# Block 0 of a fused attention and SwiGLU kernel: four unused TensorE products between q's transposes and k^T v

## The chip, the cores and the metric

The kernel runs on one core of a Trainium2 chip, in one launch. The metric is the device time of that core in microseconds. Profile times are counted from the start of the profiled execution's span. The engines are TensorE (PE for its products and transposes, PEld for its weight loads), VectorE (DVE), ScalarE (ACT), GpSimd (POOL) and SyncE (SP), which issues most DMAs.

## The reference

It is a linear attention with a norm, followed by a SwiGLU feed-forward block on the same tokens.

```
q, k, v: (8 batches, 8 heads, 576 tokens, 64)
kv  = einsum('bhsd,bhse->bhde', k, v)
out = einsum('bhsd,bhde->bhse', q, kv)
rms = sqrt(mean(out * out, axis=-1) + 1e-6)
x   = (out / rms * g_norm) as 4608 tokens x 512        (heads side by side)
g, val = x @ w_gate, x @ w_val                         (512 x 1536 each)
y   = (g * sigmoid(g) * val) @ w_out                   (1536 x 512) -> 4608 x 512
```

## The kernel before

The 4608 tokens are worked on in nine blocks of 512. A block's attention part is an `Att` object and its feed-forward part an `Ffn` object. For each batch the kernel first makes the eight matrices k^T v; then a block of q is transposed, multiplied with them, normalised and transposed again, so that x lies with its 512 columns on the partitions for the feed-forward products. Block 0 does its feed-forward products plainly (`plain_up`, line 1018). The later blocks use a scheme with seven products in place of eight, from block 2 on applied twice over (lines 549 and 712). While a block's feed-forward part runs, the attention part of the next block is slipped in between.

The weights come in 36 pieces of 0.5 MB, as pairs of 32-bit words, and are turned into float32 by ScalarE (lines 146 and 160) and VectorE (lines 147, 152, 153 and 162) while block 0 runs. They share four load buffers (`ld`) with q, k and v, so that a load waits until its buffer has been read. SyncE issues these loads in order of the program.

Block 0's attention part has nothing to run beside. Its order on each engine is the order of the program, with a few ScalarE and VectorE steps placed by hand (`tc.issue_after`). The method `first` writes it out:

- `turn_q(0, ...)`, line 335: TensorE transposes the first two of q's four tiles (four transposes each). The first result goes to a tile of `b_psum` and is copied by VectorE to `qt[:, 0]` (line 339); the second goes to `c_psum` and is copied by ScalarE (line 337).
- `first_kv`, line 248: 36 products of 64 x 64 for the first four heads and 36 for the others, in two PSUM banks, from k and v as they land. ScalarE copies one bank (line 252), VectorE adds the other (line 111).
- `product(0)`, line 355: q times k^T v for two tiles, and the squares (ScalarE, line 366) and their sums (VectorE, line 367).
- `turn_q(1, ...)`: the other two tiles of q, the same way.
- `product(1)`: the same for them.
- `warm`, line 480: seven products of 128 x 512, the identity times the turned q tile `qt[:, 3]`, into one tile of `c_psum`. Nobody reads that tile.
- `root` (lines 373 to 385) and `scale` (line 113) on VectorE: the reciprocal root by three steps of iteration, and its multiplication with the product.
- `turn_x`, line 402: TensorE transposes the normalised x, ScalarE copies it with the gain (line 403).

After this `plain_up` goes through the twelve column tiles of w_gate and w_val.

A float32 product of TensorE shows as two rows in the profile, a float32 transpose as one. `c_psum` has two buffers that are used in turn, `b_psum` three, `m_psum` two and `a_psum` one.

## Time and profile before

| what | value |
| --- | --- |
| median of 4 runs | 1031.67 us (1030.37 to 1032.05) |
| the profiled execution's own time | 1031.43 us |
| its span | 1029.5 us, so 1.93 us lie around it |
| TensorE busy (products) | 1013.5 us, 98% of the span, 8570 rows |
| VectorE busy | 703.6 us, 68% |
| ScalarE busy | 230.1 us, 22% |
| GpSimd busy | 371.3 us, 36% |
| TensorE idle from 6.81 to 10.84 us | 4.03 us |
| TensorE busy between 36 and 114.5 us | 78.50 of 78.50 us |
| DMA engines' share between 36 and 114.5 us | 0.82 |

The busy times are of one profiled execution. A row of TensorE's timeline gives the start and the duration of a group of instructions, the line of the kernel, what is written and read, the shape, and how often; the bracket tells how long the engine sat idle before it and what ended that. Durations of single rows overlap, since products are pipelined: the distance between two starts says how fast they go, the duration holds the latency too.

### The profile page before, as it was taken

The numbers are of one execution on the slowest core, as the hardware profiler recorded it, in microseconds if no ns is written. First come the engines' busy times: TensorE is split into PE (matmuls) and PEld (weight loads), VectorE is DVE, ScalarE is ACT, GpSimd is POOL, SyncE is SP. The second block draws the span as 40 slices with busy tenths as digits, with TensorE's granted clock in tenths as the row PEclk, the third lists the DMA queues.
The fourth block names the chain that finished last, engine by engine and source line by source line (L and its number), as shares of the span: only waits on it lengthen the run. The fifth ranks groups of instructions, "written<-read, shape, count | busy, mean of one in ns | idle before, by whom it ended". The sixth has DMA issues, their size and how long they took to land.

```text
span 1029.5 us, 21440 instructions
## 1 busy us (share of the span) xinstructions
PE 1013.5 (98%) x8570; PEld 904.5 (88%) x8570; DVE 703.6 (68%) x1185; ACT 230.1 (22%) x359; POOL 371.3 (36%) x280
## 2 busy tenths in 40 slices
PE   6999999999999999999999999999999999999998
PEld 4544688888999989998999899988999999989997
DVE  2999796997766855585657576674669466856661
ACT  2765121222111211211112122111112111211110
POOL 0000543444035612562156304630455136513670
PEclk9999999999999999999999999999999999999999
DMA  8689614773778466855686468736872766066601
GB/s 216 207 257 266 122 28 128 194 217 79 204 208 242 84 139 205 247 127 114 194 243 162 69 205 240 198 53 186 244 196 47 174 193 192 22 165 207 189 30 41
DMA packets 252404, 168.15 MB, mean 163 GB/s; under 512 B 129169, under 2 KB 220433, under 8 KB 252305
## 3 DMA queue, kind: packets, MB, share of 16 engines
q1 hardware_dynamic: 225808, 163.37, 58.0%
q10 hardware_dynamic: 26432, 3.41, 2.0%
q8 instruction: 68, 1.11, 0.5%
q14 instruction: 32, 0.25, 0.1%
q0 software_dynamic: 64, 0.00, 0.0%
HBM read 138.02 MB, written 22.41 MB: 156 GB/s over the span
## 4 chain that ended last, share of the span: by engine, by line
PE 83%; DVE 8%; DMA 5%; SPq 1%; ACT 1%; issue 1%; DVEq 0%; ACTq 0%
PE b L712 26%; PE b L549 20%; PE c L712 13%; PE c L549 10%; PE a L712 6%; PE a L549 5%; DMA ld<-in_moe_w_out_dram 2%; PE m L355 1%; PE m L314 1%; SPq L281 1%; DVE r L153 1%; DMA h<-in_v_dram 1%; DMA ld<-in_v_dram 1%; DVE xi L112 1%; DVE r L147 1%
## 5 line engine op out<-in xcount | busy, mean ns | idle before, releaser
L111 POOL TENSOR_TENSOR r<-r 128x256 f32<-128x256 f32 (+1 forms) x105 | 110.7, 1061 | 309.5 <-DVE r L111 206.3
L111 DVE TENSOR_TENSOR r<-b,r 128x512 f32<-128x512 f32 (+1 forms) x273 | 162.0, 606 | 64.3 <-PE b L712 59.2
L112 POOL TENSOR_TENSOR t<-wo 128x512 f32<-128x512 f32 x81 | 116.9, 1467 | 190.8 <-DVE wo L111 106.0
L111 DVE TENSOR_TENSOR r<-c,r 128x512 f32<-128x512 f32 (+1 forms) x179 | 108.4, 617 | 94.7 <-PE c L712 55.6
L712 PE MATMUL b<-x,t 128*128 128x128 f32 x1092 | 151.0, 275 | 0.0
L712 PEld LDWEIGHTS b<-x,t 128*128 128x128 f32 x1092 | 136.5, 192 | 0.6
L111 DVE TENSOR_TENSOR r<-a,r 128x512 f32<-128x512 f32 (+1 forms) x99 | 62.4, 631 | 107.9 <-PE a L549 63.0
L712 PE MATMUL c<-xi,t 128*128 128x128 f32 x840 | 112.2, 275 | 0.4 <-DVE xi L111 0.4
L113 POOL TENSOR_TENSOR h<-r 128x1024 f32<-128x1024 f32 (+1 forms) x40 | 82.1, 2069 | 80.5 <-DVE r L111 72.8
L712 PEld LDWEIGHTS c<-xi,t 128*128 128x128 f32 x840 | 102.8, 192 | 0.5 <-DVE xi L111 0.5
L549 PE MATMUL b<-wo,h 128*128 128x256 f32 x432 | 99.5, 382 | 0.1
L549 PE MATMUL b<-t,h 128*128 128x256 f32 x432 | 96.9, 381 | 0.0
L549 PEld LDWEIGHTS b<-t,h 128*128 128x128 f32 x432 | 81.4, 190 | 11.3 <-issue 0.2
L549 PEld LDWEIGHTS b<-wo,h 128*128 128x128 f32 x432 | 80.0, 190 | 12.8 <-DVE h L113 2.5
L726 ACT COPY r<-b 128x512 f32<-128x512 f32 x63 | 36.9, 585 | 211.7 <-PE b L712 199.8
L712 PE MATMUL b<-xi,t 128*128 128x128 f32 x588 | 79.7, 276 | 0.0
L712 PEld LDWEIGHTS b<-xi,t 128*128 128x128 f32 x588 | 72.4, 192 | 0.0
L712 PE MATMUL b<-x,wg 128*128 128x128 f32 x336 | 52.7, 279 | 0.2 <-DVE x L112 0.2
L712 PE MATMUL b<-x,wv 128*128 128x128 f32 x336 | 51.4, 275 | 0.0
L549 PE MATMUL c<-t,s 128*128 128x256 f32 x216 | 48.3, 380 | 0.0
L549 PE MATMUL a<-wo,h 128*128 128x256 f32 x216 | 48.3, 379 | 0.0
L549 PE MATMUL c<-wo,h 128*128 128x256 f32 x216 | 48.1, 379 | 0.0
(131 smaller groups left out, 1579.3 us busy)
## 6 DMA issues: line engine op xcount, KB each, us to landing
t<-w SPq DMA_DIRECT2D x336, 256.0 KB, 3.7
out_dram<-r SPq DMA_DIRECT2D x17, 512.0 KB, 3.1
ld<-in_k_dram SPq DMA_DIRECT2D x26, 288.0 KB, 5.0
ld<-in_v_dram SPq DMA_DIRECT2D x26, 288.0 KB, 5.7
ld<-in_moe_w_gate_dram SPq DMA_DIRECT2D x12, 512.0 KB, 4.7
ld<-in_moe_w_val_dram SPq DMA_DIRECT2D x12, 512.0 KB, 4.7
ld<-in_moe_w_out_dram SPq DMA_DIRECT2D x12, 512.0 KB, 5.2
w<-t SPq DMA_DIRECT2D x18, 256.0 KB, 2.5
```

The costliest lines, as they stand in the source:

```text
L111: add = lambda e, o, a, b: e.tensor_tensor(out=o, in0=a, in1=b, op=OP.add)
L112: sub = lambda e, o, a, b: e.tensor_tensor(out=o, in0=a, in1=b, op=OP.subtract)
L113: mul = lambda e, o, a, b: e.tensor_tensor(out=o, in0=a, in1=b, op=OP.mult)
L147: nc.vector.tensor_scalar(out=mag.bitcast(F32), in0=mag.bitcast(F32), scalar1=self.LOW, scalar2=self.HIGH, op0=OP.max, op1=OP.min,)
L153: return nc.vector.scalar_tensor_tensor(out=mag, in0=mag, scalar=3, in1=sign, op0=OP.logical_shift_left, op1=OP.bitwise_xor)
L281: nc.sync.dma_start(out=to[32 * r : 32 * (r + 1), j, g0:g1], in_=q[b, 4 * i + 2 * j + h, s0 : s0 + 32 * (g1 - g0), 32 * d : 32 * (d + 1)]. ...
L314: nc.tensor.matmul(self.kv_ps[r][u * D : (u + 1) * D, g, :], lhsT=k[:, u, c, :], rhs=v[:, u, c, :], start=(c == 0), stop=(c == KT - 1),)
L355: self.multiplied = nc.tensor.matmul(self.ps[i][u][p : p + D, t, j, :], lhsT=self.qt[rows, 2 * i + t, j, p : p + D], rhs=kvs[b % 3][rows, ...
L549: nc.tensor.matmul(banks[e][:, e], lhsT=lhsT, rhs=rhs, start=first and i == 0 and (e == 0 or banks[0] is not banks[1]), stop=i == self.ste ...
L712: nc.tensor.matmul(ps[:, i, f], lhsT=self.weight(o, p, f), rhs=self.operand(o, p), start=first and (i, f) == (0, 0), stop=True, skip_group ...
L726: nc.scalar.copy(out=dst, in_=ps)
```

## The change

`warm` gets two arguments: which of the four turned q tiles is multiplied, and how many products are made. The call after `product(1)` does what it did: seven products with `qt[:, 3]`. A new call between `turn_q(0)` and `first_kv` makes four products of 128 x 512, the identity times `qt[:, 0]`, into a tile of `c_psum` of its own. Nobody reads that tile either. On TensorE the eight rows of these four products come after q's first eight transposes and before the first product of k^T v; the order on all other engines and queues stays as it was. The numbers of all lines behind the new call go up by one.

```diff
         def first(self):
             self.turn_q(0, (b_psum, c_psum))
+            self.warm(0, 4)
             self.first_kv()
             self.product(0)
...
             with tc.issue_after(begun.ins):
                 self.product(1, (b_psum, a_psum))
-            self.warm()
+            self.warm(3, 7)
             self.root(0, 2)
...
-        def warm(self):
+        def warm(self, t, count):
 
             ps = c_psum.tile([P, NS, P], F32, name="c")
-            for _ in range(7):
-                nc.tensor.matmul(ps, lhsT=ident, rhs=self.qt[:, 3], start=True, stop=True)
+            for _ in range(count):
+                nc.tensor.matmul(ps, lhsT=ident, rhs=self.qt[:, t], start=True, stop=True)
```

## Prediction

> **What bounds the kernel now.** I read the page's chain first, then TensorE's timeline of the first 45 us, the durations of its rows by source line, the chain of waits from 13 to 31 us, and the busy time by stretch. From 36 us to 114.5 us TensorE is busy in all 78.50 of 78.50 us, and by the page's chain it carries 83% of the span. So the time is set by when that long stretch begins, and the change sits ahead of it. TensorE's timeline, with start and duration in us and the wait in brackets:

> ```profile
> 4.26 1.09 PE L335 MATMUL b<-ident,ld 128*128 128x128 f32 x4 [4.26 <-DMA ld<-in_q_dram]
> 5.70 1.11 PE L335 MATMUL c<-ident,ld 128*128 128x128 f32 x4 [0.35 <-DMA ld<-in_q_dram]
> 10.84 2.40 PE L248 MATMUL m<-h 64*64 64x64 f32 x72 [4.03 <-DMA h<-in_v_dram]
> 13.94 2.42 PE L248 MATMUL m<-h 64*64 64x64 f32 x72 [0.70 <-DMA h<-in_v_dram]
> ...
> 22.68 6.37 PE L480 MATMUL c<-r,ident 128*128 128x512 f32 x14
> 28.89 1.04 PE L402 MATMUL m<-ident,r 128*128 128x128 f32 x8
> ```

> The new products go between the second and the third line, into a hole of 4.03 us that ends when k and v land. A product of 128x512 is two rows here: L480's seven give x14.

> Next, row durations by source line (min/median/max in ns, first and last start). L248 and L314 are the same kind of product (k^T v), in block 0 and in the later blocks; L480 is the unused product:

> ```profile
> L248 PE MATMUL m<-h x144: 310/311/365, 10.8 to 16.0; 64*64 64x64 f32 x144
> ...
> L314 PE MATMUL m<-xi x72: 218/218/268, 114.6 to 115.7; 64*64 64x64 f32 x72
> ...
> L480 PE MATMUL c<-r,ident x14: 592/592/790, 22.7 to 28.5; 128*128 128x512 f32 x14
> ```

> The same row takes 311 ns early and 218 later. 72 of them are issued in 2.10 us early (13.94 to 16.04) and in 1.09 us later (L314's two batches start at 114.60 and 115.69). Transposes are issued every 0.213 us at L335 and every 0.109 us at L402 (eight starts from 28.89 to 29.65). So TensorE runs at half speed at first. The turn lies inside the first row of L480: it starts at 22.68, its successor at 23.31, all later ones 0.43 apart. The column of granted clock doesn't show it; it reads 1.00 (after the engines' busy times) in the stretch that holds the 311 ns rows too:

> ```profile
> 13.90:16.40 2.50, 2.42 (x72) 2.26 (x72) 0.00 (x0) 0.37 (x1) 0.00 (x0) 1.00 1.08 283
> ```

> Last, the chain of waits from 13 to 31 us:

> ```profile
> 4.96 8.84 DMA h<-in_v_dram
> 13.80 0.14 issue
> 13.94 2.44 PE m L248 x72
> ...
> 16.48 0.44 DVE kv L111
> ...
> 16.96 1.98 PE m L355 x64
> 18.94 1.04 PE b L335 x4
> 19.98 0.87 PE c L335 x4
> 20.87 0.58 ACT r L337
> 21.46 0.58 ACT r L146
> ...
> 22.06 0.43 DVE r L147
> ```

> v lands at 13.80, and from there to 20.9 us the path is half-speed work of TensorE, then VectorE's. That half-speed work is what four products in the hole can touch.

> **The change, part by part.** *Added: 8 rows on TensorE and one tile of c_psum.* They need qt[:, 0], copied by VectorE in the 0.69 us from 5.38, so nothing holds them after the last transpose: they start at about 6.39 + 0.21 = 6.60. At full speed 8 rows are 8 x 0.43 = 3.4 us; at half speed, with the ratio of the transposes (0.213/0.109), an estimate of 0.85 each, 6.8 us: an end between 10.0 and 13.4. Queued behind them is the first batch of L248, ready at 10.84.

> *When the clock opens.* By the rows it opened, before, about 6 us into work that had no break since 16.96; counted from the first batch at 10.84, over breaks of 0.70 and 0.60, about 12 us. The new unbroken work starts with the transposes at 5.70. By the first count it opens near 11.8, by the second near 17. I take the first, since the old work with breaks had not opened the clock by 16.4, 5.5 us in. Then six rows run slowly to 11.7, two fast to 12.6; the first batch of L248 takes 1.09 us to 13.7, and the second starts at 13.94 as before: v's landing hides the delay of the first batch. If the clock opens earlier there is only more idle time ahead of 13.94.

> [...]

> *What gets faster from 13.94 on.* (1) Second batch of L248: ScalarE's copy of the first bank at 16.01 follows a row issued about 1.68 us into the batch; 1.68 x (1 - 1.09/2.10) = 0.81, plus 0.09 of shorter latency (311 to 218): 0.9 us. (2) product(0), 16.96 to 18.87: 16 groups of four rows, 0.107 apart now and 0.06 at 123.4 to 124.0; 16 x 0.062 + 0.1 = 1.09 for 1.91: 0.8 us. (3) The first four transposes of turn_q(1): three steps of 0.104, and the latency 421 to 273 ns: 0.46 us. Sum at VectorE's copy (20.02): 2.18 us.

> [...]

> *VectorE's chain.* From 20.02 to 35 us it is nearly without a break; its 0.16 us wait for ScalarE ahead of 22.06 goes too, since the last four transposes give ScalarE another 0.4 us. VectorE gains 2.18 + 0.16 = 2.34 us.

> *What could be late next.* Piece 0 of the weights is issued at 10.76 and lands 6.5 us later, at 17.3; ScalarE's L146 wants it at 21.36 - 2.5 = 18.9. The q tiles 2 and 3, issued at 7.11 and 7.52, land in 7.8 and 8.3 us, at 15.8 by the later; turn_q(1) would want them at 17.1. Piece 1 lands 5.9 us after 13.55, at 19.5, and is wanted at 21.8. All are in time by over 1 us. Piece 3 waits for turn_q(1) to free its buffer (SyncE's queue, issued at 20.87), so it moves up with it; no other DMA is passed.

> *The seven products of L480* end at 28.9 now, just behind the scale of VectorE that ends at 28.53. They would end near 25.5 (14 x 0.43 after 19.5), the scale at 26.2: the transposes L402 start there, 2.6 us earlier, waiting for VectorE. After that VectorE (wv at 32.9) and ScalarE's x copies, bound to it, let TensorE's long stretch start 2.3 to 2.6 us earlier. A second path reaches 122 us just behind TensorE: weights, then v, then the q loads of SyncE (last issue 119.71, landing in 2.16), and TensorE waits 0.20 us for their transpose. It starts at VectorE's releases, so I give it VectorE's 2.34.

> Tile order on every other engine stays as it is; the extra c tile only exchanges which of two buffers each later tile gets, and the new tile has no reader. I price that at zero: its writer is TensorE itself, long done. Its cover gone, a later writer would wait for a c tile's copy, 0.6 us.

> **Sum.** The profiled execution took 1031.43 us, a span of 1029.5 and 1.93 around it. Less 2.35 it is 1029.1 us. The median is 1031.67, 0.24 above that execution; from there it would be 1029.3. A measurement of this kernel can tell about 0.2% from no change, 2.06 us, so the forecast stands just beyond that bound.

> **Rivals.**
> - *The clock opens too late, and the products delay k^T v* (the slower one). All 8 rows at half speed end at 13.4; the first batch then runs to 15.5, the second starts at 15.55 in place of 13.94: 1.6 us later. If all up to 22 us stays slow, the time is 1033.0 us. It decides from an opening after about 17.4 us, where (2) and (3) no longer pay for the 1.6 us. For it: the count of 12 us. Against it: five to six us of unbroken work sufficed.
> - *It opens in between* (12.5 to 17): part of L248 is slow, and 0.3 to 2 us are gained: 1029.4 to 1031.1, middle 1030.3.
> - *It opens and closes again.* With an early opening TensorE idles up to 1.4 us before 13.94, then 0.8 us behind the second batch. No idle time after 22.9 in this trace is over 0.4 us, so it shows nothing of that. What follows would be slow again, and the gain zero: 1031.4 us.
> - *The gain is lost later.* Between 36 and 114.5 us the DMA engines are 82% busy; if the loads keep their own pace, the second path takes back more than half: 1030.4 us.

> **How the numbers follow.** The forecast has 0.69, the slower rival 0.07, the opening in between 0.12, the closing 0.06, the loss later 0.06. The forecast's own range is 1028.2 to 1029.9: the bounds of (1) to (3) and of the paths behind (a gain of 1.9 to 2.8), and the 0.24 us to the median. To hold 8 in 10 it reaches over the in-between case and the loss later: 1028.2 to 1031.0. Faster by over 0.2%, so below 1029.6, holds four fifths of the forecast and a little of the in-between case: 0.60. Slower by over 0.2%, above 1033.7, needs the first rival and a second mishap: 0.05. The rest is 0.35.

> **What would show it.** Right: eight rows of c<-r,ident from 6.6 us, the first ones about 0.85 apart, the last ones 0.43; rows of L248 at 218 ns from 13.94; L335's second group at 273 ns; VectorE's copy near 17.8; L402 near 26.3; the long stretch 2.3 to 2.6 us earlier. Wrong: rows of L248 at 311 ns and a start of the second batch after 14.2 (the first two rivals); 218 ns, then 311 again (the third); all of it right by 40 us and the wait ahead of 123 us grown (the fourth).

## The result and the profile after

The changed kernel takes 1033.2 us (median of 42 runs, 1031.04 to 1041.03), the kernel before 1031.48 us in the runs beside it (60 runs, 1029.87 to 1033.36). The ratio is 1.0017, with a 95% interval of 1.0012 to 1.0022: slower by 1.7 us, where 2.4 us less were forecast. The profiled execution took 1034.69 us, with a span of 1032.6 us.

TensorE's timeline of the changed kernel (start, duration, operation, and in brackets the idle time before it):

```profile
6.85 4.61 PE L481 MATMUL c<-r,ident 128*128 128x512 f32 x8
11.39 1.38 PE L248 MATMUL m<-h 64*64 64x64 f32 x72
14.07 1.40 PE L248 MATMUL m<-h 64*64 64x64 f32 x72 [1.30 <-DMA h<-in_v_dram]
16.20 1.15 PE L355 MATMUL m<-kv,r 64*64 64x64 f32 x61 [0.73 <-DVE kv L111]
20.68 0.48 PE L355 MATMUL m<-kv,r 64*64 64x64 f32 x3 [3.34 <-issue]
21.09 1.11 PE L335 MATMUL b<-ident,ld 128*128 128x128 f32 x4
...
24.90 6.78 PE L481 MATMUL c<-r,ident 128*128 128x512 f32 x14
31.52 1.04 PE L402 MATMUL m<-ident,r 128*128 128x128 f32 x8
```

The first four lines are the forecast. The eight rows fit into the hole, the 72 rows of a batch of k^T v take 1.4 us in place of 2.4, and product(0) begins at 16.20 in place of 16.96, although v landed 0.13 us later. Then TensorE stops for 3.34 us, three rows before the end of product(0). The releaser is "issue": nothing that the profile shows was being waited for. The three rows behind the stop read the same tiles, q's turned one and k^T v, as rows ahead of it.

The clock is the second surprise. The busy time by stretch (TensorE's products, weight loads, VectorE, ScalarE, GpSimd; then granted clock, DMA share and GB/s):

```profile
15.70:19.12 3.42, 1.15 (x61) 1.01 (x61) 0.42 (x1) 0.00 (x0) 0.00 (x0) 1.00 1.04 345
19.12:22.53 3.41, 1.85 (x10) 1.73 (x11) 0.29 (x1) 1.08 (x2) 0.00 (x0) 0.50 0.12 34
22.53:25.94 3.41, 3.41 (x69) 2.44 (x68) 3.21 (x7) 2.08 (x4) 0.00 (x0) 0.50 0.49 140
25.94:29.36 3.42, 3.42 (x9) 1.52 (x8) 3.04 (x13) 1.83 (x4) 0.00 (x0) 1.00 0.46 140
```

It closes at 19.12, when the stop has lasted 1.8 us, and opens again at 25.94. So what follows the stop runs at half speed like before: the transposes, product(1), and the first rows of the seven unused products, which take 6.78 us for 6.37. VectorE's copy and its scale come late by the same 2.2 us (20.02 and 27.24 before):

```profile
22.24 0.69 DVE L339 COPY r<-b 128x512 f32<-128x512 f32 x1 [6.10 <-PE b L335]
...
29.47 1.29 DVE L113 TENSOR_TENSOR r<-m,y 128x512 f32<-128x512 f32 x2
```

The transposes L402 start 2.63 us later than before (31.52 for 28.89), and the feed-forward products behind them 2.62 us later (32.89 for 30.27). That is most of the 3.1 us by which the span grew; where the rest arises was not looked into.

The view of DMA queues has a line that I had not used: packets of kind "instruction" (queue and kind, then packets, MB, share). In the changed kernel one such packet starts at 18.11 us; this is the stretch from 18.05 to 18.20:

```profile
q8 instruction: 1, 0.02, 46.8%
```

In the kernel before the corresponding packet starts at 16.02 (16.0 to 16.1 us):

```profile
q8 instruction: 1, 0.02, 60.4%
```

It carries 16384 bytes and takes about 1 us on its DMA engine (60.4% of 16 engines in 0.1 us are 0.97 us, 46.8% in 0.15 us are 1.12). I take queue q8 for TensorE's, since its packets go with TensorE's rows in number: 68 in the kernel before, for 8570 products and transposes and as many weight loads, and 67 in the run e1 below, for 8450. TensorE goes on at 20.68, 2.57 us after the packet's start. **Theory:** TensorE had used up the instructions it held, and the next 16 KB had been delayed among 1.5 MB of weight loads. **Rivals:** a wait bound to a place in product(0), or the clock closing by itself.

### The profile page after: what moved, and what is told of

Same layout as the page of the kernel before. It is cut to its first block, busy times and chain, and to the rows that moved or that the text cites. A ratio compares the mean times of both kernels' runs of the same rounds, so it can differ in the third digit from the quotient of the medians.

```text
span 1032.6 us, 21456 instructions
## 1 busy us (share of the span) xinstructions
PE 1015.5 (98%) x8578; PEld 904.0 (88%) x8578; DVE 703.8 (68%) x1185; ACT 230.1 (22%) x359; POOL 371.3 (36%) x280
## 3 DMA queue, kind: packets, MB, share of 16 engines
q10 hardware_dynamic: 26432, 3.41, 2.0%
q8 instruction: 68, 1.11, 0.5%
## 4 chain that ended last, share of the span: by engine, by line
PE 84%; DVE 7%; DMA 5%; SPq 1%; issue 1%; ACT 1%; ACTq 0%; DVEq 0%
PE b L713 26%; PE b L550 20%; PE c L713 13%; PE c L550 10%; PE a L713 6%; PE a L550 5%; DMA ld<-in_moe_w_out_dram 2%; PE m L355 1%; PE m L314 1%; SPq L281 1%; DVE r L153 1%; DMA h<-in_v_dram 1%; DMA ld<-in_v_dram 1%; DVE xi L112 1%; DVE r L111 1%
## 5 line engine op out<-in xcount | busy, mean ns | idle before, releaser
L111 POOL TENSOR_TENSOR r<-r 128x256 f32<-128x256 f32 (+1 forms) x105 | 110.7, 1061 | 309.3 <-DVE r L111 233.9
L111 DVE TENSOR_TENSOR r<-b,r 128x512 f32<-128x512 f32 (+1 forms) x273 | 162.0, 606 | 64.3 <-PE b L713 59.1
L111 DVE TENSOR_TENSOR r<-c,r 128x512 f32<-128x512 f32 (+1 forms) x179 | 108.4, 617 | 95.1 <-PE c L713 55.6
L111 DVE TENSOR_TENSOR r<-a,r 128x512 f32<-128x512 f32 (+1 forms) x99 | 62.4, 631 | 107.8 <-PE a L550 62.9
```

The lines of the kernel that those rows point to most:

```text
L111: add = lambda e, o, a, b: e.tensor_tensor(out=o, in0=a, in1=b, op=OP.add)
```

## The experiments

What the profiles of all runs show: the start of the packet, the row of TensorE after which it stopped without a wait that the profile shows (its products and transposes, counted from the start), where the clock closes again after its first opening, and the profiled execution's own time:

| run | packet starts | stop without a shown wait | clock closes | profiled execution | median |
| --- | --- | --- | --- | --- | --- |
| before | 16.02 | none | no | 1031.43 | 1031.5 |
| changed | 18.11 | row 221, 3.34 us | 19.1 | 1034.69 | 1033.2 |
| fewer rows (e1) | 17.44 | none | 23.3 | 1033.43 | 1035.15 |
| fewer rows, without the four products (e1) | 19.65 | none | no | 1037.69 | 1038.45 |
| changed, again (e7) | 16.47 | row 221, 1.77 us | 20.2 | 1032.26 | - |
| six products (e2) | 19.22 | row 221, 2.39 us | 22.4 | 1034.17 | 1033.76 |
| ten small products more (e6) | 16.50 | row 221, 1.79 us | 20.3 | 1032.08 | 1030.17 |
| two loads held (e5) | 16.34 | row 221, 1.80 us | no | 1030.6 | 1031.57 |
| three loads held (e3) | 15.67 | row 221, 0.60 us | no | 1029.7 | 1029.81 |
| the same again (e9) | 15.10 | row 221, 0.40 us | no | 1028.59 | 1029.15 |
| held, ten small ones more (e8) | 15.04 | row 221, 0.15 us from start to start | no | 1029.23 | 1030.02 |
| held, without the four products (e4) | 15.38 | none | no | 1031.8 | 1031.8 |

**Fewer instructions ahead (e1, two runs).** The edit, in the run with the four products; its partner lacks them. The seven unused products are kept behind product(1) in both.

```diff
-                    for r in range(2) if c < T else (g,):
-                        for u in range(2):
-                            ...
+                    for u in range(2):
+                        h = 2 * j + u
+                        rows = slice(0, P) if c < T else slice(g * D, (g + 1) * D)
+                        k, v = (t[c][rows, h if c < T else h % NS] for t in (self.k, self.v))
+                        ... nc.tensor.matmul(banks[0 if c < T else 1 + g][u * D : (u + 1) * D, j], ...)
...
-                        for p in range(p0, p1, D):
+                        w = D if self.n else P
+                        for p in range(p0, p1, w):
```

> The changed kernel with fewer TensorE instructions ahead of the long stretch: k^T v takes 128 rows of tokens per product in place of two products of 64 (the last 64 tokens go to a bank of their own, so VectorE adds two halves), and block 0's q products take 128 tokens in place of two of 64. TensorE then has 8 + 8 + 80 + 32 + 8 + 32 = 168 product rows ahead of the seven unused products, where the changed kernel stopped for 3.34 us after 221. Theory (TensorE ran out of loaded instructions, the next 16 KB came too late): no stop of over 0.5 us before the seven products, clock open from about 9 us on and not closed again, VectorE's copy of the turned q near 18 us, time 2 to 2.8 us below its partner without the four products, about 1029. Rival (the stop belongs to a place in product(0), a PSUM bank or a semaphore): the stop stays, and so does a time of 1032 to 1033.5. Rival (a busy TensorE closes its own clock): clock closes near 19 us whether it stops or not.

> Partner of the run above: the same fewer instructions, without the four products. All theories: the time of the kernel before within 0.5 us (VectorE's second half-add costs 0.2 us), half speed up to 20 to 24 us. Only the difference to its partner is at stake: theory of the instructions 2 to 2.8 us, the rivals -1 to +0.5 us.

Measured: 1035.15 us with the four products (12 runs, 1031.05 to 1037.82) and 1038.45 without (5 runs, 1036.86 to 1038.73). One of the first run's expectations holds: no stop without a shown wait. TensorE's timeline of the run with the products:

```profile
16.23 2.00 PE L359 MATMUL m<-kv,r 64*128 64x64 f32 x32 [0.54 <-DVE kv L111]
18.16 0.66 PE L338 MATMUL b<-ident,ld 128*128 128x128 f32 x4
...
20.82 0.32 PE L359 MATMUL b<-kv,r 64*128 64x64 f32 x1 [1.57 <-DVE r L342]
```

The others fail. VectorE's copy comes at 20.09, not near 18, since VectorE is at its sums of squares until then; the clock closes at 23.3 us, behind the wait of 1.57 us for that copy; and the time is 6 us above the 1029 expected. The partner is 7 us slower than the kernel before, where 0.5 was allowed. Most of that is there at the transposes of x (34.72 for 28.89): product(0) takes 3.68 us for 32 wide rows, where 64 rows took 1.98, product(1) takes 1.7 us longer too, and the clock opens only at 29.78. The early products gain 3.3 us here, beyond the 2 to 2.8 expected, but the base is another, and the number is not to be carried over.

```profile
17.62 3.68 PE L359 MATMUL m<-kv,r 64*128 64x64 f32 x32 [0.39 <-DVE kv L111]
```

**Six products (e2).** `self.warm(0, 6)` in place of `self.warm(0, 4)`.

> Six products in place of four in the hole, 12 rows in place of 8. Theory of the instructions: TensorE stops after the same number of product rows, 221, that is after 57 of product(0)'s 64 in place of 61, and resumes when the instruction packet has come, 2.3 to 2.8 us after that packet's start. Rival (a place in the code): it stops after 61 rows again. The rows end near 13.3 us, so the second batch of k^T v starts up to 0.4 us later; time 1033 to 1033.8 by both.

1033.76 us (10 runs); ratio to before 1.0019 (1.0011 to 1.0028). TensorE's timeline:

```profile
18.11 1.08 PE L355 MATMUL m<-kv,r 64*64 64x64 f32 x57 [0.76 <-DVE kv L111]
21.58 0.34 PE L355 MATMUL m<-kv,r 64*64 64x64 f32 x7 [2.39 <-issue]
```

57 rows, then the stop. 8 + 12 + 144 + 57 is 221, as 8 + 8 + 144 + 61 is. The stop is tied to the number of instructions, and the rival of a place in product(0) is out. One part of the expectation fails: in this profile the clock opens only at 12.12, the twelve rows end near 14.9 in place of 13.3, and the second batch of k^T v starts at 16.02, 1.9 us later than in the changed kernel (14.07).

**Weight loads held (e3).** SyncE's first three weight loads wait for VectorE's sum of k^T v; the order on the other engines stays.

```diff
-            add(nc.vector, kvs[0], banks[1], kvs[0])
+            made = add(nc.vector, kvs[0], banks[1], kvs[0])
+            load_weights(4)
+            for piece in pieces[:3]:
+                tc.add_manual_dep(words[piece].sent.ins, made.ins.name, ...)
...
-    load_weights(4)
```

> The changed kernel, but SyncE's first weight load waits for VectorE's sum of k^T v (about 16.1 us) in place of being issued at 10.8 us; two more loads follow it. Nothing else is moved. Theory of the instructions, with the packet held up behind the weight loads in the DMA engines: the instruction packet starts before 16.5 us (18.1 with the loads), the stop shrinks from 3.34 us to under 1.3 us, the clock stays open; piece 0 of the weights then lands near 20 us and holds VectorE by about 1 us; time 1030 to 1031.5. If the packet's time depends on TensorE's progress alone: it starts near 18 us, the stop stays over 3 us, and the time is 1033 to 1034.

1029.81 us (10 runs, 1029.13 to 1030.64), ratio 0.9985 (0.9976 to 0.9994), a little below the range expected. The packet starts at 15.67, the stop is 0.60 us, and the clock stays open:

```profile
16.66 1.15 PE L361 MATMUL m<-kv,r 64*64 64x64 f32 x61 [0.73 <-DVE kv L111]
18.41 0.33 PE L361 MATMUL m<-kv,r 64*64 64x64 f32 x3 [0.60 <-issue]
```

I had expected piece 0 to be late by 1 us; ScalarE did not wait for it. A second set on another chip (e9) gave 1029.15 us (8 runs, 1028.2 to 1031.24), ratio 0.9978 (0.9969 to 0.9988): 2.2 us below the kernel before, again a little below the range, and the fastest version here.

> The kernel of e3_late_weights again, on the same chip as e8_late_more and in more rounds: 1029.3 to 1030.3 us, a stop of 0.4 to 0.8 us after row 221, clock open.

**Weight loads held, without the four products (e4).** The same edit in the kernel before.

> The kernel before (without the four products) with the weight loads held until VectorE's sum of k^T v, as in the run e3_late_weights. Theory: without the early products TensorE is at half speed up to 20 us and does not run out of instructions in either order of loads, so holding the loads brings nothing by itself: 1031 to 1032.5 us, clock open near 20 to 24 us. If it is the loads' order that gained in e3_late_weights: about 1029.8 here too.

1031.8 us (11 runs), ratio 1.0003 (0.9993 to 1.0012). The order of the loads gains nothing by itself, so the gain of e3 and e9 is that of the early products, let through.

**Two loads held (e5).** Piece 0 is loaded as in the kernel before; `pieces[1:3]` wait.

> The changed kernel, with piece 0 of the weights loaded as early as before and only pieces 1 and 2 held until VectorE's sum. Theory: the instruction packet has 0.5 MB of weights ahead of it in place of 1.5 or none, so it starts between 15.7 and 17.2 us, and the stop after row 221 lies between 0.6 and 2 us; time 1029.5 to 1031.5. Rival (only the order of issue counts, not the bytes in flight): packet near 18 us, 1033 us.

1031.57 us (11 runs), ratio 0.9997 (0.9988 to 1.0006), the packet at 16.34, the stop 1.80 us. The packet is later than in all four profiles with three loads held (15.04 to 15.67), but not earlier than in all those with none held (16.02 to 19.65). The median is 0.07 us beyond the range.

**The changed kernel again (e7).**

> The changed kernel once more, for a second profile. Theory: TensorE stops after row 221 again; the length of the stop follows the instruction packet's start (resuming 2.3 to 2.8 us after it), which may differ from 18.1 us by a microsecond or two, and the time follows the stop, 1031 to 1036 us. Rival (a fixed wait in the code): 3.3 us again.

The stop is 1.77 us, so the rival of a fixed wait fails; it follows the packet (16.47, and TensorE goes on 2.52 us later). e7 and e5 have stops of the same length, but the clock closes in e7 alone. The stretches are cut where it changes; first e7, then e5:

```profile
16.75:20.16 3.41, 1.64 (x43) 1.38 (x32) 0.22 (x1) 0.87 (x2) 0.00 (x0) 1.00 0.77 255
20.16:23.58 3.42, 3.12 (x67) 2.30 (x66) 3.25 (x7) 2.24 (x5) 0.00 (x0) 0.50 0.48 155
```

```profile
17.53:20.94 3.41, 1.83 (x43) 1.53 (x47) 1.23 (x3) 1.88 (x4) 0.00 (x0) 1.00 0.90 271
20.94:24.35 3.41, 3.41 (x55) 1.91 (x47) 3.34 (x8) 3.06 (x6) 0.00 (x0) 1.00 0.57 163
```

In e7 the stop lies in one stretch of 3.41 us, which is busy for 1.64 us of it; in e5 it falls on two, and the emptier is busy for 1.83 us. Both start product(0) near 16 us (16.07 and 15.81), and the transposes L402 come at 29.18 in e7 and at 28.11 in e5: less the 0.26 us, about 0.8 us are left for the closed clock, an estimate from one profile of each.

**Ten small products more (e6, e8).** Products of 64x64 behind the four, in the changed kernel and in that of e3.

```diff
+            for _ in range(10 if t == 0 else 0):
+                nc.tensor.matmul(ps[0:D, 0, 0:D], lhsT=ident[0:D, 0:D], rhs=ident[0:D, 0:D], ...)
```

> The changed kernel with ten small unused products of 64x64 (20 rows) behind the four. The instruction count then says: TensorE stops after row 221 again, which is now row 41 of product(0) (8 + 8 + 20 + 144 + 41). If the request for the next 16 KB is made when TensorE passes a fixed instruction, near row 97 as in e1 (row 97 was row 9 of the second batch of k^T v, past 14.1 us, and is now row 61 of the first batch, about 13 us): the packet starts about 1 us earlier than the 18.1 of the changed kernel, so at about 17, stop of 2 to 3 us. If the request does not hang on that row: packet near 18.1 again, stop of 3.5 to 4 us. Time 1032 to 1034 by both.

> The changed kernel with both: the weight loads held until VectorE's sum of k^T v (e3_late_weights), and ten small unused products of 64x64 behind the four (e6_more_rows). Theory: TensorE passes the row that requests the next 16 KB near 13.2 us in place of 14.6, with no weight load in the packet's way it starts near 14.3, and TensorE comes to row 221 near 17.3 us with the instructions there or up to 0.3 us short of them; clock open throughout; time 1028.8 to 1029.6 us. If the request does not move with the row: packet near 15.7, stop of 0.9 to 1.3 us, time 1029.8 to 1030.6.

In e6 TensorE stops after row 41 of product(0), row 221 again:

```profile
16.24 0.85 PE L355 MATMUL m<-kv,r 64*64 64x64 f32 x41 [0.75 <-DVE kv L111]
18.89 0.57 PE L355 MATMUL m<-kv,r 64*64 64x64 f32 x23 [1.79 <-issue]
```

The packet starts at 16.50, near the expected 17, but e7 has 16.47 without these products; so it doesn't show that the request moves with a row. The stop is 1.79 us, below both expectations. In e8 the packet starts at 15.04, between the 14.3 and the 15.7 of the two expectations. Which instruction triggers the request stays open.

Product(0) of e8 seems to have no stop, since the view merges its 64 rows into one line. Asked for in two stretches, it shows a short one at the same place, behind 41 rows:

```profile
16.70 0.85 PE L361 MATMUL m<-kv,r 64*64 64x64 f32 x41 [0.75 <-DVE kv L111]
```

```profile
17.48 0.57 PE L361 MATMUL m<-kv,r 64*64 64x64 f32 x23
```

Row 221 starts at 17.33 and row 222 at 17.48, 0.15 us later, where the rows of one group start 0.007 us apart; 17.48 is 2.44 us after the packet. The durations of the rows overlap, so that a stop this short doesn't count as idle time.

The medians are 1030.17 us in e6 (10 runs, 1029.08 to 1033.83; ratio to before 0.9991, 0.998 to 1.0003) and 1030.02 in e8 (12 runs, 1028.73 to 1032.95; 0.9991, 0.9983 to 1.0). e6 is below the range of both expectations; e8 is above the first and inside the second, whose stop of 0.9 to 1.3 us did not come.

**The clock in all executions.** e6 gains 3 us over the changed kernel in its median, which its own profiled execution (1032.08) doesn't show. The granted clock that is on record for each execution, as a mean over the span, explains that. In the profiles here it reads 0.999 or 1.000 where the clock stays open, and 0.998 or 0.997 where it closes for 3.4 or 6.8 us. Executions and their median times by it:

| kernel | clock stays open | clock closes again |
| --- | --- | --- |
| changed | 2: 1031.85 | 40: 1033.25 |
| fewer rows (e1) | 2: 1031.45 | 10: 1035.68 |
| six products (e2) | none | 10: 1033.76 |
| two loads held (e5) | 4: 1030.48 | 7: 1031.69 |
| ten small products more (e6) | 6: 1029.85 | 4: 1032.38 |
| held, ten small ones more (e8) | 9: 1029.70 | 3: 1032.27 |
| three loads held (e3, e9) | 16: 1029.50 | 2: 1030.62 |

The profiled execution of e6 is one of the four. In the profiles with a stop behind row 221 the clock closed with stops of 1.77 to 3.34 us and stayed open with stops of 0.15 to 1.80, so the difference between the columns is the price of both. That ten small products keep the clock open in 6 of 10 executions, where the changed kernel has 2 of 42, suggests that they shorten the stop in most executions; how is not shown.

## Why the prediction was wrong

**The hole.** Right. The clock opened at 8.88 us, inside the third row (its start is 8.56, the next 9.15), not near 11.8, and in the runs with four or six products between 8.9 and 12.1. That is 2.94 us into the unbroken work that began with the transposes at 5.94, where my count from one opening had about 6 us; in e2 it is 5.90 us (6.22 to 12.12).

**The terms.** Term (1), 0.9 us: from the start of the second batch to that of product(0) it was 3.02 us and is 2.13, so 0.89. Term (2), 0.8 us: product(0) to the transposes was 1.91. In e8 it is 1.29 (16.70 to 17.99), which still has the short stop in it: 0.14 us, and 0.05 for the slower start behind it, where two groups are 0.09 us apart in place of 0.04. Without them it is 1.10, so the term was 0.81. Term (3), 0.46 us: transposes to VectorE's copy was 1.15 and is 0.69 in e8, so 0.46. So transposes do run faster once the clock is open (272 ns in e8 for 417 in the kernel before); whether transposes count as work that opens the clock, no run here tests. The sum is 2.16 us for 2.18. One bound does not follow from its own numbers: a gain of at most 2.8 us leads to 1028.6, not to the 1028.2 of the range.

**The step that failed** is "What could be late next". It looked at what TensorE's rows read (weights, q tiles) and at what frees their buffers, and took all to be in time by over 1 us. It left out what, by the theory, TensorE itself needs: its next 16 KB of instructions. In the kernel before, row 221 starts at 19.78, 3.8 us after the packet's start, and in the runs with a stop TensorE went on 2.3 to 2.7 us after such a start: an estimated cover of 1.1 to 1.5 us, made of half-speed rows. With the change row 221 starts at 17.1, by faster rows and by eight more of them. The packet starts no earlier for that (16.5 to 18.1 in the two profiles), and TensorE stops for 1.77 to 3.34 us; where the loads ahead of the packet are held, 0.60 and 0.40 us are left (e3, e9), and the time falls below that of the kernel before.

**The rivals.** The time of the slower rival (1033.0) was met by luck: in the changed kernel's profile the products delayed nothing. Only the six of e2 delayed the second batch, by 1.9 us. "It opens and closes again" did happen, and I gave it 0.06 and a gain of zero, where 1.7 us were lost. I had looked at the idle time around the second batch, which came out as 1.30 us before it and 0.73 behind it; these did not close the clock. It closed inside the stop (at 19.12, in the stop from 17.34 to 20.68), and where the stop was short (0.15 to 0.60 us) it stayed open, which speaks against a clock that closes by itself. In e9 the clock stays open, VectorE's copy starts at 18.34 us, and L402 2.16 us earlier than before:

```profile
15.84 1.15 PE L361 MATMUL m<-kv,r 64*64 64x64 f32 x61 [0.73 <-DVE kv L111]
17.39 0.33 PE L361 MATMUL m<-kv,r 64*64 64x64 f32 x3 [0.40 <-issue]
...
26.73 1.06 PE L408 MATMUL m<-ident,r 128*128 128x128 f32 x8 [0.28 <-DVE r L113]
```

There the forecast's path holds to the end: 2.16 us at L402, 2.2 us in the median.

**The price of the stop.** Between the changed kernel and e9, VectorE's copy differs by 3.90 us (22.24 and 18.34): 2.94 is the longer stop, 0.36 the later start of product(0), and 0.60 the half-speed rows behind the stop. Up to L402 the difference grows to 4.79 us (31.52 and 26.73); product(1) and the first unused products at half speed stand in that stretch.

**How far it is shown.** That TensorE stops at a fixed count of rows is shown (row 221 in eight profiles, which is row 41, 57 or 61 of product(0); each stop ends 2.3 to 2.7 us after the start of a packet). That it had run out of instructions there is my reading of the two together. That weight loads hold the packet up rests on 15.0 to 15.7 us in four profiles with the loads held, 16.3 in one with one load ahead, and 16.0 to 19.7 in seven with three. What else moves it by up to 3.6 us is open: the changed kernel alone had 18.11 and 16.47. How the 1.7 us of the median divide between stop and clock is open too; the clock closed in 40 of 42 executions, and the two others (1031.62 and 1032.08) were not faster than the kernel before.

## What to carry to other kernels

Before making an engine faster in a stretch with dense DMA, look up the instruction packets in the view of DMA queues, and ask when the faster engine comes to the row that stood behind such a packet. Here row 221 came at 17.1 us in place of 19.78, while the packet started at 18.11 and 16.47 in place of 16.02. If a stop named "issue" moves in the code when you add rows (row 61, 57 and 41 of product(0) here), and its place in rows counted from the start doesn't (row 221), suspect the loading of the code, and try to hold back the loads that nobody needs yet: here the stop went from 3.34 and 1.77 us to 0.60 and 0.40, and the median from 1033.2 us to 1029.81 and 1029.15. Work that opens the clock was worth less here where the clock closed again behind a stop: 1033.25 us for 1031.85 in the changed kernel, 1030.62 for 1029.50 with three loads held. And before a median is explained by one profile, look whether the granted clock of the other executions is that of the profiled one (in e6 it was 0.998 in the profiled one and 1.000 in six of ten).
